# One 8 MB K load per group into a buffer of three 32 KB thirds, with P·V one group later, in a decode attention kernel

## The chip, the core and the metric

The kernel runs on one NeuronCore of a Trainium2 chip. Five engines execute their own instruction lists and meet at semaphores: TensorE (PE: matmuls, with PEld its weight loads), VectorE (DVE), ScalarE (ACT), GpSimd (POOL) and SyncE (SP), which here only starts transfers. Sixteen DMA engines move data between HBM and the on-chip memory SBUF (128 partitions); TensorE writes to PSUM. The metric is the device time of one execution in microseconds (us); lower is better.

## The reference

One decode step for 8 sequences (`B`), model width 576, 32 heads of 128 channels, a cache of 4096 keys and values per head, in bf16. An attention branch and an MLP branch are mixed by a gate:

```python
q = (x @ wq).reshape(B, Sq, H, Dh)                       # 576 -> 32*128, Sq = 1
scores = einsum("bhqd,bhkd->bhqk", q, k_cache) * (Dh ** -0.5)
p = softmax(scores); o = einsum("bhqk,bhkd->bhqd", p, v_cache)
a = o.reshape(B, Sq, H * Dh) @ wo                        # 4096 -> 576
b = gelu(layernorm(x) @ w1 + b1) @ w2 + b2               # 576 -> 4608 -> 576
g = sigmoid((x * gate_w).sum(-1)); out = g * a + (1 - g) * b
```

K and V are 8 x 32 x 4096 x 128 bf16 values each, 268 MB each; the weights are some 20 MB together. Every byte of them is used once.

## The kernel before

**Groups.** The 256 pairs (sequence, head) are worked in 32 groups (`NG`) of 8 heads of one sequence. In a group, partition p holds 256 consecutive keys (`NTT`) of one head: 16 partitions (`RH`) per head, and 256 keys x 128 channels x 2 bytes = 64 KB per partition, contiguous in HBM. So K of a group is 128 rows of 64 KB, 8 MB, and V the same.

**A group's work.** `scores` goes through 8 chunks of 32 keys (`CT`). `mult` (line 443) multiplies a chunk of K by the broadcast query on DVE into one of two buffers `p1`; eight matmuls with the identity (lines 454 and 179) add the products up in PSUM to 16 partial sums per key; `reduce` (line 461) adds those on DVE into `s_sb`. `softmax` takes the maximum on DVE (lines 478 to 486), the exponential on ACT (`E`, line 487), spreads it over the 8 heads into `P` (line 490), and sums it (lines 493 and 494). On PE, `total` (line 511) adds the sums over partitions, and `pv` (line 504, 64 matmuls) multiplies `P` by V. `evict` (line 516) copies the result by ACT, `gather` (line 522) folds it on PE, `norm` (lines 527 and 528) divides on DVE, and `put` (line 436) stores it for the output projection.

**Buffers.** `KB` is two buffers of 32 KB per partition, one for each half of a group's keys; `VB` holds one group's V (64 KB); `RB` (41,472 bytes) holds wq, then w2, then wo. w1 lies in `VB` until V of group 0 comes.

**Order.** Each engine's list is in the order in which the Python code appends to it (`op`; `aside` puts an instruction on the engine's second semaphore). All large loads are started by SP, in its order, and run on one DMA queue: wq, w1, both K halves of group 0, w2 (after the q projection, `p_Q`), V of group 0 (after the up projection has read w1, `p_up`). Then, in each group n, `load_k` of the two halves of group n+1, each waiting until the last `mult` on its half of group n (`k_done`), and `load_v` of group n+1, which waits until `pv` of group n is done (`v_done`). wo is loaded in group 0, after the down projection. Within group n the order on PE is `scores`, `total`, `pv`, `gather`, all of group n; `norm` of group n runs on DVE inside `scores` of group n+1. The up projection (line 542, 216 matmuls) runs on PE ahead of group 0; `act_h` (ACT and POOL, lines 549 to 557) makes `hT_sb` of it; the down projection (line 566, 144 matmuls) runs between the chunks of group 0. `Stream.emit_loop` writes groups 1 to 29 of PE and DVE as loops of one group each.

**The end.** V of the last group comes in eight parts, one of 128 keys in `KB[0]` and seven small ones in `VB`, and P·V follows them part by part; then the last quarter of the output projection (`a_proj`, line 566), the mix (line 691) and four small stores.

Of the kernel before, what the change touches and what calls it, by code (L numbers as in the profile page):

```python
# [12 lines left out]
B = 8  # L13
D = 576
# [126 lines left out]
def bass_gated_mix__mha_block_cached__mixer_channel_mlp__decode_kernel(  # L141
# [46 lines left out]
    wq_sb = view(RB, 0, [128, 4, SK])  # L188
    wq_t = view(RB, 4 * SK, [128, SK // 2])
    w1_sb = view(VB, 0, [128, 4, F])  # L190
    w1_t = view(VB, 4 * F, [128, F // 2])
    w2_sb = view(RB, 0, [128, NJ, D])
    wo_sb = view(RB, 0, [128, H, D])
# [63 lines left out]
    sK = [nc.alloc_semaphore(f"sK{i}") for i in range(2)]  # L257
    sV = nc.alloc_semaphore("sV")
    nK, nV = [0, 0], [0]
# [16 lines left out]
    def halves(w):  # L276
# [5 lines left out]
    ld_w1 = [load("sync", w1_sb, B_w1[0:512, :].rearrange("(p kt) f -> p kt f", kt=4), "ld_w1a"),  # L282
             load("sync", w1_t, halves(B_w1), "ld_w1b")]
# [9 lines left out]
    def load_k(u):  # L293
        n, s = divmod(u, NKH)
        nK[s] += 1
        src = kv_src(A_k_cache, n)[:, s * NTK:(s + 1) * NTK, :]
        k_land[u] = op("sync", lambda e: e.dma_start(KB[s][:, :, :], src), [k_done.get(u - NKH)], dma=(sK[s], 16 * nK[s]))

    def load_v(n):
        nV[0] += 1  # L300
        src = kv_src(A_v_cache, n)
        t = op("sync", lambda e: e.dma_start(VB[:, :, :], src), [v_done.get(n - 1) if n else st["p_up"]], dma=(sV, 16 * nV[0]))  # L302
        v_land[n] = [(t, VB, 0, 0, NTT)]
# [8 lines left out]
    V_LAST = (32, 32, 16, 16, 16, 8, 8)  # L312
    T_TURN = NTK + 64

    load_k(0)
    load_k(1)
# [13 lines left out]
    def blank(ps):  # L330
# [4 lines left out]
    c_selO = op("vector", lambda e: e.tensor_reduce(  # L335
        out=selO[:].rearrange("p t h -> p h t"),
        in_=bass.AP(tensor=ident, offset=0, ap=[[pstride(ident), 128], [TQ, HB], [1, TQ], [32, 4]]),
        axis=AX.X, op=ALU.add), [c_id])
# [38 lines left out]
    def untransposed(dst, col, waits):  # L377
# [9 lines left out]
    v_omg = op("vector", lambda e: e.tensor_scalar(out=stat[:, OMG_COL:OMG_COL + 1], in0=stat[:, G_COL:G_COL + 1],  # L387
                                                   scalar1=-1.0, scalar2=1.0, op0=ALU.mult, op1=ALU.add), [a_g])
    for i in range(4):
        a_g4 = aside("scalar", lambda e, i=i: e.activation(out=g4[32 * i:32 * i + B, :], in_=stat[:, G_COL:G_COL + 2],  # L390
                                                        func=ACT.Copy), [v_omg, c_g4])
# [6 lines left out]
    for half in range(2):  # L398
        for h in range(4):
            for kt in range(NKT):  # L400
                o = tr_ps[half][32 * h:32 * h + B, :]
                at = (kt * SK + half * (SK // 2) if kt < NKF else NKF * SK) + h * DH
                r = bass.AP(tensor=RB, offset=at, ap=[[pstride(RB), 128], [4 * DH, 4], [1, DH]])
# [8 lines left out]
    last = NG - 1  # L412
    AP = 30
    LOOP = {"tensor": 1, "vector": 1}
# [24 lines left out]
    def mult(n, c):  # L439
        u, par = n * NKH + c // NCK, c % 2  # L440
        t0 = (c % NCK) * CT
        qb = bass.AP(tensor=q_n, offset=0, ap=[[pstride(q_n), 128], [0, CT], [1, DH]])
        v_mult[n, c] = op("vector", lambda e: e.tensor_tensor(  # L443
            out=p1[:, par, :, :], in0=KB[u % NKH][:, t0:t0 + CT, :], in1=qb, op=ALU.mult),
            [k_land[u], a_q[n], p_sum.get((n, c - 2) if c >= 2 else (n - 1, c + NC - 2))]
            + ([v_yT, p_yT, p_Q] if n == 0 and c < 2 else []))
        if c % NCK == NCK - 1:
            k_done[u] = v_mult[n, c]
        for i in range(NCH):
            r = bass.AP(tensor=p1, offset=p1[:, par, 0, i * CH:i * CH + 1].offset,  # L450
                        ap=[[pstride(p1), 128], [DH, CT], [1, CH]])
            w = [v_mult[n, c], v_red.get((n, c - 2) if c >= 2 else (n - 1, c + NC - 2)), *a_Q] if i == 0 else ()
            if i == 0:
                fn = lambda e, r=r: e.matmul(tr_ps[par][:, :], lhsT=ident[:, :], rhs=r, start=True, stop=False)  # L454
            else:
                fn = lambda e, r=r, i=i: held(e, tr_ps[par][:, :], ident[:, :], r, i == NCH - 1)
            p_sum[n, c] = op("tensor", fn, w)

    def reduce(n, c):
        par = c % 2  # L460
        v_red[n, c] = op("vector", lambda e: e.tensor_reduce(  # L461
            out=s_sb[:, c * CT:(c + 1) * CT], in_=tr_ps[par][:, :].rearrange("p (t c) -> p t c", c=CH),
            axis=AX.X, op=ALU.add), [p_sum[n, c], a_exp.get(n - 1)])
# [71 lines left out]
    def up_proj(j0, j1):  # L535
        for jt in range(j0, j1):
            for kt in range(NKF + 2):
# [3 lines left out]
                w = bass.AP(tensor=VB, offset=at, ap=[[pstride(VB), 128], [NJ, n]])  # L541
                st["p_up"] = aside("tensor", lambda e, w=w, o=o, kt=kt: e.matmul(  # L542
# [3 lines left out]
    def act_h():  # L546
        hb, t2 = (up[:, i, :] for i in range(2))
        b1b = bass.AP(tensor=b1_sb, offset=0, ap=[[pstride(b1_sb), 128], [1, NJ], [0, B]])
        t = aside("scalar", lambda e: e.activation(out=hb, in_=up_ps[:, 0:NJ * B], func=ACT.Copy), [st["p_up"]])
# [6 lines left out]
        t = aside("scalar", lambda e: e.activation(out=t2, in_=t2, func=ACT.Sigmoid, scale=gelu_c), [t])  # L556
# [6 lines left out]
    def quarters(lhsT, w, first, stop, waits):  # L563

        for i in range(4):
            last = aside("tensor", lambda e, i=i: e.matmul(  # L566
                y_ps[32 * i:32 * i + B, 0:QN], lhsT=lhsT, rhs=w[:, i * QN:(i + 1) * QN], start=first, stop=stop),
                waits if i == 0 else ())
        return last
# [7 lines left out]
    def down_proj(j0, j1):  # L577
        for jt in range(j0, j1):
            st["p_down"] = quarters(hT_sb[:, jt, :], w2_sb[:, jt, :], jt == 0, jt == NJ - 1,
                                    [st["ld_w2"], st["v_h"], c_yps] if jt == 0 else ())  # L580

    def b_out():
        st["a_bx"] = aside("scalar", lambda e: e.activation(
            out=bmg_sb[0:QP, :], in_=y_ps[0:QP, 0:QN], func=ACT.Copy), [st["p_down"], st["v_h"]])
# [7 lines left out]
    def load_wo():  # L592
        st["ld_wo"] = load("sync", wo_sb, A_wo.rearrange("(h d) n -> d h n", d=128), "ld_wo", [st["p_down"]])
# [25 lines left out]
    done_a = [0]  # L619
    for b in range(B):  # L620
        q_of(b)
        if b == 0:
            q_group(0)
        up_proj(b * NJ // B, (b + 1) * NJ // B)
    act_h()
    load_w2()
    load_v(0)
    for n in range(NG):
        for e, l0 in LOOP.items():
            if l0 <= n <= AP:  # L630
                S.marks.setdefault(e, []).append(len(S.ops[e]))

        def between(c, n=n):
            if c == 1 and 1 <= n < last:
                norm(n - 1)
            if n == last and c == NCK:
                load_v_part(n, KB[0], 0, 0, NTK, [k_done[NKH * n]])
                t0 = NTK
                for nt in V_LAST:
                    load_v_part(n, VB, t0 - NTK, t0, t0 + nt, [p_pv[n - 1]])  # L640
                    t0 += nt
            if n == 0 and 3 <= c <= 6:
                down_proj((c - 3) * NJ // 4, (c - 2) * NJ // 4)
            if n >= AP and c % NCK == 2 and done_a[0] < NHG - 1:
                a_proj(done_a[0])
                done_a[0] += 1

        scores(n, between)
        if n < last:
            q_group(n + 1)  # L650
        softmax(n)
        if n < last:
            total(n)
        if n < last - 1:
            load_k(NKH * (n + 1))
            load_k(NKH * (n + 1) + 1)
            pv(n, (0,))
            evict(n)
            gather(n)
            if n == 0:  # L660
                b_out()
                load_wo()
            if n + 1 < last - 1:
                load_v(n + 1)
        if n == last - 2:
            load_v_part(last - 1, VB, 0, 0, NTK, [v_done[n]])
        if n == last - 1:
            load_k(NKH * last)
            load_k(NKH * last + 1)
            load_v_part(n, VB, NTK, NTK, NTT, [v_done[n - 1]])  # L670
            pv(n, (0,))
# [3 lines left out]
    pv(last - 1, (1,))  # L675
    evict(last - 1)
    gather(last - 1)
    norm(last - 1)
# [7 lines left out]
    pv_turned(last, range(4, 1 + len(V_LAST)))  # L686
    norm_turned(last)
    while done_a[0] < NHG:
        a_proj(done_a[0])
        done_a[0] += 1  # L690
# [48 lines left out]
```

## Time and profile before

| | us |
|---|---|
| median of 3 runs | 1302.52 (1301.04 to 1302.96) |
| the profiled execution: its time | 1302.29 |
| its span, first to last instruction | 1299.1 |
| DVE busy | 849.8 (65%) |
| PE busy | 813.6 (63%) |
| ACT busy | 68.7 (5%) |
| moved | 557.14 MB, mean 429 GB/s |

The time is 3.2 us above the span, so a change of the span is read as a change of the time. The profile gives for each engine its busy time, for each DMA queue the packets, bytes and the time that its packets took as a share of sixteen engines' span, and for each group of instructions (line, engine, operation, tile) the busy time, the mean of one and what ended the idle time before it. A row of the timeline has its start in us from the span's start, its length, the engine, the line, what is written and read, a count, and in brackets the engine's idle time before it and what ended that.

### The profile page before, as it was taken

To read this page: it belongs to the slowest core of one execution; us is meant where nothing else is said; L and a number is where in the kernel's file an instruction comes from. 1 tells how busy PE (TensorE), PEld (TensorE's weight loads), DVE (VectorE), ACT (ScalarE), POOL (GpSimd) and SP (SyncE) were. 2 spreads that over 40 slices of the span, in tenths; PEclk is the share of its full clock that TensorE was granted. 3 is DMA by queue.
4 is the path that set the end of the run, shared out by engine and by line. 5 is a ranking of instruction groups with operands and counts; after the bars stand their busy time and mean duration, and the time that the engine had idled before them with its cause. 6 is when DMAs were issued, how large, how long until landed. Compare 5 with 4: busy or idle time off the path is not lost.

```text
span 1299.1 us, 10783 instructions
## 1 busy us (share of the span) xinstructions
PE 813.6 (63%) x5020; PEld 166.9 (13%) x3228; DVE 849.8 (65%) x1073; ACT 68.7 (5%) x158; POOL 6.1 (0%) x19
## 2 busy tenths in 40 slices
PE   3963666566666565756665765665665566666667
PEld 2410111100111110111110111110011110011112
DVE  1455666677666668666668666668766667766685
ACT  3100000000000000000000000000000000000000
POOL 0100000000000000000000000000000000000000
PEclk8678877888877898888889888889878888978888
DMA  9999999999999999999999999999999999999997
GB/s 405 434 418 422 447 426 438 418 435 435 438 438 428 425 435 434 442 428 430 430 433 433 438 430 440 421 434 429 440 438 426 435 424 435 436 434 438 419 434 335
DMA packets 20124, 557.14 MB, mean 429 GB/s; under 512 B 2048, under 2 KB 6160, under 8 KB 7056
## 3 DMA queue, kind: packets, MB, share of 16 engines
q1 hardware_dynamic: 19840, 556.94, 99.7%
q8 instruction: 8, 0.13, 0.0%
q10 hardware_dynamic: 272, 0.04, 0.0%
q14 instruction: 4, 0.03, 0.0%
HBM read 556.96 MB, written 0.01 MB: 429 GB/s over the span
## 4 chain that ended last, share of the span: by engine, by line
DMA 67%; DVE 18%; PE 11%; issue 3%; SPq 0%; DVEq 0%; ACT 0%
DMA KB<-in_A_k_cache_dram 63%; DVE p L443 15%; PE psb L179 7%; DVE s_sb L461 2%; DMA VB<-in_B_w_dram 2%; DMA VB<-in_A_v_cache_dram 2%; PE psb L542 2%; PE psb L454 1%; DVEq L134 0%; SPq L262 0%; PE psb L504 0%; PE psb L421 0%; SPq L302 0%; DVE P L490 0%; PE psb L566 0%
## 5 line engine op out<-in xcount | busy, mean ns | idle before, releaser
L443 DVE TENSOR_TENSOR p<-KB,q_n 128x4096 bf16<-128x4096 bf16 x256 | 581.9, 2283 | 310.5 <-DMA KB<-in_A_k_cache_dram 301.5
L179 PE MATMUL psb<-p,ident 128*128 128x512 bf16 x1792 | 483.9, 415 | 0.0
L454 PE MATMUL psb<-p,ident 128*128 128x512 bf16 x256 | 110.7, 433 | 270.8 <-DVE p L443 270.7
L461 DVE TENSOR_REDUCE s_sb<-psb 128x32 f32<-128x512 f32 x256 | 175.2, 684 | 92.7 <-PE psb L179 92.7
L504 PE MATMUL psb<-VB,P 128*32 128x512 bf16 x1984 | 177.0, 535 | 12.0 <-DMA VB<-in_A_v_cache_dram 12.0
L454 PEld LDWEIGHTS psb<-p,ident 128*128 128x128 bf16 x256 | 26.1, 102 | 723.8 <-DVE p L443 633.4
L511 PE MATMUL psb<-rs,ones 128*128 128x8 f32 x64 | 18.9, 368 | 155.3 <-DVE rs L494 155.3
L504 PEld LDWEIGHTS psb<-VB,P 128*32 128x32 bf16 x1984 | 64.5, 129 | 110.9 <-issue 94.7
L490 DVE TENSOR_SCALAR P<-E,own 128x256 bf16<-128x256 bf16 x248 | 51.9, 284 | 17.9 <-ACT E L487 17.9
L522 PE MATMUL psb<-selO,O_sb 128*128 128x8 f32 x256 | 33.9, 259 | 22.8 <-ACT O_sb L516 22.8
L511 PEld LDWEIGHTS psb<-rs,ones 128*128 128x128 f32 x64 | 15.9, 308 | 212.0 <-DVE rs L494 211.3
L431 ACT ACTIVATE q_n<-q_bc 128x128 bf16<-128x128 bf16 x32 | 9.9, 309 | 551.1 <-DVE p L443 551.1
L522 PEld LDWEIGHTS psb<-selO,O_sb 128*128 128x128 f32 x256 | 31.0, 191 | 38.2 <-ACT O_sb L516 38.2
L516 ACT ACTIVATE O_sb<-psb 128x512 f32<-128x512 f32 x32 | 19.1, 596 | 275.6 <-PE psb L504 275.6
L487 ACT ACTIVATE E<-s_sb,mD 128x256 bf16<-128x256 f32 x32 | 16.2, 507 | 145.4 <-DVE mD L486 145.4
L542 PE MATMUL psb<-yT_sb,VB 128*128 128x8 bf16 (+1 forms) x216 | 20.1, 230 | 6.0 <-issue 6.0
L542 PEld LDWEIGHTS psb<-yT_sb,VB 128*128 128x128 bf16 (+1 forms) x216 | 18.4, 166 | 10.4 <-issue 9.3
L436 ACT ACTIVATE OT_sb<-O_n 128x8 bf16<-128x8 bf16 x31 | 7.4, 237 | 212.0 <-DVE O_n L528 212.0
L478 DVE TENSOR_REDUCE mA<-s_sb 128x1 f32<-128x256 f32 x32 | 13.4, 420 | 1.1
L493 DVE TENSOR_REDUCE es<-E 128x1 f32<-128x256 bf16 x32 | 13.2, 411 | 0.0
L494 DVE TENSOR_SCALAR rs<-own,es 128x8 f32<-128x8 f32 x32 | 7.4, 231 | 1.1
L373 PE MATMUL psb<-ident,p 8*128 8x8 bf16 x12 | 0.7, 168 | 11.7 <-ACT p L366 11.7
(75 smaller groups left out, 102.2 us busy)
## 6 DMA issues: line engine op xcount, KB each, us to landing
KB<-in_A_k_cache_dram SPq DMA_DIRECT2D x64, 4096.0 KB, 26.8
VB<-in_A_v_cache_dram SPq DMA_DIRECT2D x2, 4096.0 KB, 24.1
RB<-in_B_w_dram SPq DMA_DIRECT2D x1, 5184.0 KB, 40.2
VB<-in_B_w_dram SPq DMA_DIRECT2D x1, 4608.0 KB, 23.9
RB<-in_A_wo_dram SPq DMA_DIRECT2D x1, 4608.0 KB, 39.7
RB<-in_A_wq_dram SPq DMA_DIRECT2D x1, 4096.0 KB, 12.6
KB<-in_A_v_cache_dram SPq DMA_DIRECT2D x1, 4096.0 KB, 15.9
VB<-in_A_v_cache_dram SPq DMA_DIRECT2D x2, 1024.0 KB, 19.0
```

Source lines behind the costliest of these rows:

```text
L179: return e.add_instruction(mybir.InstMatmult(name=nc.get_next_instruction_name(), engine=mybir.EngineType.PE, ins=[e.lower_ap(rhs), e.lowe ...
L443: v_mult[n, c] = op("vector", lambda e: e.tensor_tensor(out=p1[:, par, :, :], in0=KB[u % NKH][:, t0:t0 + CT, :], in1=qb, op=ALU.mult), [k_ ...
L454: fn = lambda e, r=r: e.matmul(tr_ps[par][:, :], lhsT=ident[:, :], rhs=r, start=True, stop=False)
L461: v_red[n, c] = op("vector", lambda e: e.tensor_reduce(out=s_sb[:, c * CT:(c + 1) * CT], in_=tr_ps[par][:, :].rearrange("p (t c) -> p t c" ...
L478: t = op("vector", lambda e: e.tensor_reduce(out=mA[:, 0:1], in_=s_sb[:, :], axis=AX.X, op=ALU.max), [v_red[n, NC - 1], c_mA])
L487: a_exp[n] = op("scalar", lambda e: e.activation(out=E[:, :], in_=s_sb[:, :], func=ACT.Exp, bias=mD[:, 0:1], scale=1.0), [v_nm[n], v_P.get ...
L490: v_P[n] = op("vector", lambda e, h=h: e.tensor_scalar(out=(P if n < NG - 1 else P_last)[:, :, h, :], in0=E[:, :].rearrange("p (q t) -> p ...
L504: p_pv[n] = op("tensor", lambda e, o=o, tq=tq, at=at, buf=buf: e.matmul(o, lhsT=(P if n < last else P_last)[:, tq, :, :].rearrange("p h t ...
L511: p_z[n] = op("tensor", lambda e: e.matmul(oz_ps[:, HB:2 * HB], lhsT=ones[:, :], rhs=rs[:, :], start=True, stop=True), [v_rs[n], v_norm.ge ...
L516: a_ev[n] = op("scalar", lambda e: e.activation(out=O_sb[:].rearrange("p t d -> p (t d)"), in_=o_ps[n // last][:, :], func=ACT.Copy), [p_p ...
L522: p_oz[n] = op("tensor", lambda e, tt=tt: e.matmul(o, lhsT=O_sb[:, tt, :], rhs=selO[:, tt, :], start=(tt == 0 and n < last), stop=(tt == T ...
L542: st["p_up"] = aside("tensor", lambda e, w=w, o=o, kt=kt: e.matmul(o, lhsT=w, rhs=yT_sb[:, kt, :], start=(kt == 0), stop=(kt >= NKF)), [*l ...
```

## The change

- **K buffer.** `KB` and `RB` become one tensor `KR`: three thirds of 32 KB, of which the third one is the first part of the region of 41,472 bytes. K of group n is one load of 8 MB, 64 KB per partition, into two neighbouring thirds: thirds 0 and 1 for odd n and for n = 0, thirds 1 and 2 for the other even n (`k_base`). Third 1 is shared by all groups; `scores` reads the half that lies there first (`k_order`), and `load_k(n + 1)` waits for the last `mult` on it. Group 0 is still loaded in two halves.
- **V and P one group later.** In group n PE runs `scores(n)`, then `total`, `pv` and `gather` of group n-1; `load_v(n)` waits for `pv(n - 1)`. DVE runs `softmax(n)`, then `norm(n - 1)`; on ACT `evict(n - 1)` stands ahead of the exponential of group n.
- **The head.** SP starts wq, the two K halves of group 0, then w1. wq lies in `VB`, w1 in the region behind thirds 0 and 1, w2 in `VB` behind the first 88 tokens. V of group 0 comes in two loads: the first 88 tokens after `p_Q`, the other 168 after the down projection. The up projection, `act_h` and the down projection follow `scores(0)` on PE, in one piece each.
- **The end.** wo is loaded after the last `mult` of group 30 into the region where w1 was; the first three quarters of `a_proj` run after `scores(31)`. V of group 31 comes in the same eight parts, but into thirds 0 and 1, after the last `mult` of group 31.
- **Loops.** PE's loop covers groups 1 to 30, DVE's loop the same in turns of two groups.

```diff
-    KB = [sb(f"KB{i}", [128, NTK, DH], BF16) for i in range(NKH)]
+    THIRD = NTK * DH
+    RB0 = 2 * THIRD
+    KR = sb("KR", [128, RB0 + 9 * F // 2], BF16)
     VB = sb("VB", [128, NTT, DH], BF16)
-    RB = sb("RB", [128, 9 * F // 2], BF16)
...
+    V_AHEAD = 88
+    w2_sb = view(VB, V_AHEAD * DH, [128, NJ, D])
+    wo_sb = view(KR, RB0, [128, H, D])
+    VL = view(KR, 0, [128, NTT, DH])
...
+    def k_base(n):
+        return THIRD if n % 2 == 0 and n > 0 else 0
+    def k_order(n):
+        return (n % 2, 1 - n % 2)
+    def load_k(n):
+        nK[0] += 1
+        waits = [k_done[0, 1]] if n == 1 else [k_done[n - 1, k_order(n - 1)[0]], st["p_up"]]
+        dst = view(KR, k_base(n), [128, NTT, DH])
+        t = op("sync", lambda e: e.dma_start(dst, kv_src(A_k_cache, n)), waits, dma=(sK, 16 * nK[0]))
+        k_land[n, 0] = k_land[n, 1] = t
...
-    load_k(0)
-    load_k(1)
+    load_k_half(0, 0)
+    load_k_half(0, 1)
+    ld_w1 = [load("sync", w1_sb, ...
...
-    LOOP = {"tensor": 1, "vector": 1}
+    LOOP = {"tensor": 1, "vector": 2}
...
     def load_wo():
-        st["ld_wo"] = load("sync", wo_sb, A_wo.rearrange("(h d) n -> d h n", d=128), "ld_wo", [st["p_down"]])
+        st["ld_wo"] = load("sync", wo_sb, A_wo.rearrange("(h d) n -> d h n", d=128), "ld_wo", [k_done[last - 1, 1]])
...
         scores(n, between)
         if n < last:
             q_group(n + 1)
+            load_k(n + 1)
+        if n == 0:
+            load_v(0, 0, V_AHEAD, [p_Q])
+            up_proj(0, NJ)
+            softmax(0)
+            act_h()
...
+            down_proj(0, NJ)
+            b_out()
+            load_v(0, V_AHEAD, NTT, [st["p_down"]])
+            continue
+        if n == last - 1:
+            load_wo()
+        total(n - 1)
+        if n == last:
+            for hg in range(NHG - 1):
+                a_proj(hg)
+        pv(n - 1, (0,))
+        evict(n - 1)
+        gather(n - 1)
+        if n < last:
+            load_v(n)
         softmax(n)
...
+        norm(n - 1)
...
+    for nt in V_LAST:
+        load_v_part(last, VL, t0, t0, t0 + nt, [k_done[last, 0]])
```

More of the change, by code (lines that the diff above doesn't have):

```diff
@@ L255, in bass_gated_mix__mha_block_cached__mixer_channel_mlp__decode_kernel @@
     YT_COL = 64
-    sK = [nc.alloc_semaphore(f"sK{i}") for i in range(2)]
+    sK = nc.alloc_semaphore("sK")
     sV = nc.alloc_semaphore("sV")
-    nK, nV = [0, 0], [0]
+    nK, nV = [0], [0]
     def load(engine, dst, src, name, waits=()):
@@ L310, in load_v_part @@
         v_land.setdefault(n, []).append((t, buf, at - t0, t0, t1))
-    V_LAST = (32, 32, 16, 16, 16, 8, 8)
+    V_LAST = (128, 32, 32, 16, 16, 16, 8, 8)
     T_TURN = NTK + 64
-    load_k(0)
-    load_k(1)
+    last = NG - 1
+    load_k_half(0, 0)
+    load_k_half(0, 1)
+    ld_w1 = [load("sync", w1_sb, B_w1[0:512, :].rearrange("(p kt) f -> p kt f", kt=4), "ld_w1a"),
+             load("sync", w1_t, halves(B_w1), "ld_w1b")]
     def memset(engine, ap, value):
@@ L460, in reduce @@
         par = c % 2
+        at = (k_order(n)[c // NCK] * NCK + c % NCK) * CT
         v_red[n, c] = op("vector", lambda e: e.tensor_reduce(
-            out=s_sb[:, c * CT:(c + 1) * CT], in_=tr_ps[par][:, :].rearrange("p (t c) -> p t c", c=CH),
+            out=s_sb[:, at:at + CT], in_=tr_ps[par][:, :].rearrange("p (t c) -> p t c", c=CH),
             axis=AX.X, op=ALU.add), [p_sum[n, c], a_exp.get(n - 1)])
@@ L561, in load_w2, with quarters @@
         st["ld_w2"] = load("sync", w2_sb, B_w2.rearrange("(p j) n -> p j n", j=NJ), "ld_w2", [p_Q])
-    def quarters(lhsT, w, first, stop, waits):
+    def quarters(lhsT, w, first, stop, waits, end=aside):
         for i in range(4):
-            last = aside("tensor", lambda e, i=i: e.matmul(
+            last = (end if i == 3 else aside)("tensor", lambda e, i=i: e.matmul(
                 y_ps[32 * i:32 * i + B, 0:QN], lhsT=lhsT, rhs=w[:, i * QN:(i + 1) * QN], start=first, stop=stop),
@@ L616, in norm_turned @@
             [p_oz[n], v_rz[n]])
[L619 to L625, printed above, removed]
+    q_of(0)
+    q_group(0)
     load_w2()
-    load_v(0)
     for n in range(NG):
-        for e, l0 in LOOP.items():
-            if l0 <= n <= AP:
+        for e, turn in LOOP.items():
+            if n >= 1 and (n - 1) % turn == 0:
                 S.marks.setdefault(e, []).append(len(S.ops[e]))
         def between(c, n=n):
[L634 to L646, printed above, removed]
+            if n == 0 and c + 1 < B:
+                q_of(c + 1)
         scores(n, between)
@@ L650, in bass_gated_mix__mha_block_cached__mixer_channel_mlp__decode_kernel @@
             q_group(n + 1)
-        softmax(n)
[L652 to L671, printed above, removed]
+            load_k(n + 1)
[4 more added lines that the diff above has]
+            act_h()
+            c_selO = op("vector", lambda e: e.tensor_reduce(
+                out=selO[:].rearrange("p t h -> p h t"),
+                in_=bass.AP(tensor=ident, offset=0, ap=[[pstride(ident), 128], [TQ, HB], [1, TQ], [32, 4]]),
+                axis=AX.X, op=ALU.add), [c_id])
+            v_omg = op("vector", lambda e: e.tensor_scalar(out=stat[:, OMG_COL:OMG_COL + 1], in0=stat[:, G_COL:G_COL + 1],
+                                                           scalar1=-1.0, scalar2=1.0, op0=ALU.mult, op1=ALU.add), [a_g])
+            for i in range(4):
+                a_g4 = aside("scalar", lambda e, i=i: e.activation(out=g4[32 * i:32 * i + B, :], in_=stat[:, G_COL:G_COL + 2],
+                                                                func=ACT.Copy), [v_omg, c_g4])
+            down_proj(0, NJ)
[13 more added lines that the diff above has]
+            load_v(n)
+        softmax(n)
+        norm(n - 1)
         if n == last - 4:
@@ L674, in bass_gated_mix__mha_block_cached__mixer_channel_mlp__decode_kernel @@
             b_gate()
[L675 to L678, printed above, removed]
+    t0 = 0
+    for nt in V_LAST:
+        load_v_part(last, VL, t0, t0, t0 + nt, [k_done[last, 0]])
+        t0 += nt
     pv(last, (0,))
@@ L685, in bass_gated_mix__mha_block_cached__mixer_channel_mlp__decode_kernel @@
     gather(last)
-    pv_turned(last, range(4, 1 + len(V_LAST)))
+    pv_turned(last, range(4, len(V_LAST)))
     norm_turned(last)
-    while done_a[0] < NHG:
-        a_proj(done_a[0])
-        done_a[0] += 1
+    a_proj(NHG - 1)
     t = op("vector", lambda e: e.scalar_tensor_tensor(
```

66 lines of the change are left out of this document (27 added, 39 removed).

## The prediction

> **What bounds the kernel now.** I read the profile's page first for the shares and the DMA queue, then one row over 25 groups of the steady part, then the DMA rows of stretches in which only K or only V is in flight, then one group's timeline.
>
> ```profile
> span 1299.1 us, 10783 instructions
> ...
> q1 hardware_dynamic: 19840, 556.94, 99.7%
> ...
> DMA 67%; DVE 18%; PE 11%; issue 3%; SPq 0%; DVEq 0%; ACT 0%
> ...
> L443 DVE TENSOR_TENSOR p<-KB,q_n 128x4096 bf16<-128x4096 bf16 x256 | 581.9, 2283 | 310.5 <-DMA KB<-in_A_k_cache_dram 301.5
> ...
> L542 PE MATMUL psb<-yT_sb,VB 128*128 128x8 bf16 (+1 forms) x216 | 20.1, 230 | 6.0 <-issue 6.0
> ...
> KB<-in_A_k_cache_dram SPq DMA_DIRECT2D x64, 4096.0 KB, 26.8
> ...
> VB<-in_A_v_cache_dram SPq DMA_DIRECT2D x30, 31.5
> ```
>
> The load queue's packets fill 99.7% of sixteen engines' span. DVE's `mult` waits 301.5 us for K. A K half takes 26.8 us from issue to landing, and V 31.5.
>
> ```profile
> core 0: us, PE busy (x) PEld busy (x) DVE busy (x) ACT busy (x) POOL busy (x), PEclk, DMA share, GB/s
> 256.70:1226.10 969.40, 608.88 (x3450) 108.92 (x2050) 660.10 (x825) 41.27 (x100) 1.15 (x2) 0.85 1.00 433
> ```
>
> These 969.40 us are 25 groups (100 ACT instructions, four a group): 38.776 us a group, the DMA engines at a share of 1.00 and 433 GB/s. PE has 24.4 us of matmuls a group and DVE 26.4. So the transfers bound the kernel: a change of the other engines' work is worth nothing here by itself, and what counts is the time that the queue's packets take, and whether the queue ever runs dry.
>
> **The packets: the only term of the sum.** K comes in 32 KB packets (a half's row of a partition), V in 64 KB ones. 128 rows over 16 engines make 16 K and 8 V packets per engine and group. Three stretches with only K in flight, then three with only V, 15 us each:
>
> ```profile
> DMA packets 217, 6.59 MB, mean 439 GB/s; under 512 B 16, under 2 KB 16, under 8 KB 16
> ...
> q1 hardware_dynamic: 217, 6.59, 102.0%
> ```
>
> ```profile
> q1 hardware_dynamic: 218, 6.62, 102.5%
> ```
>
> ```profile
> q1 hardware_dynamic: 210, 6.36, 98.5%
> ```
>
> ```profile
> q1 hardware_dynamic: 96, 6.29, 96.9%
> ```
>
> ```profile
> q1 hardware_dynamic: 97, 6.36, 97.9%
> ```
>
> (One V row stands for two stretches that read alike.) 15 us of 16 engines are 240 us. K: 1.020, 1.025 and 0.985 of that are 727.2 us, for 217+218+210 packets less 16 tiny ones each, the completion writes: 597, so 1.2181 us each. V: 2 x 232.56 + 234.96 us for 289, 2.4224 us each. Two K packets cost 2.4362, one V packet of the same bytes 2.4224: 14 ns less. Checked against the clock: 16 x 1.2181 + 8 x 2.4224 = 38.869 us for a period of 38.776, so neighbours overlap by 0.093 us over 24 packets, 3.9 ns each. With K in 64 KB packets a group has 16 of them: 16 x (2.4224 - 0.0039) = 38.696. That is 0.080 us less per group, and 31 groups (1 to 31; group 0 stays in halves) give 2.5 us. V of group 30 becomes one load and V of group 0 two, which cancels; w1, w2, wo and the last V parts keep their rows. Shares are rounded to 0.1%, so at worst each stretch is off by 0.12 us of its 240, the K packet by 0.0006 us and the V packet by 0.0012; with the overlap fitted again to the period, the saving is 1.9 to 3.1 us. I take the middle, 2.5.
>
> The Trainium skill, in "DMA: Bandwidth & Descriptors", section "Why small descriptors are slow (HBM only)", gives a fixed overhead of about 3 cycles per packet; at the 850 MHz of its section "Where 436 GB/s comes from" that is 3.5 ns, by estimate 8 x 31 x 3.5 ns = 0.9 us in place of 2.5. The rows above show about 10 ns a packet, so I go by them.
>
> **Does the queue stay fed?** Everything else in the change is free as long as each load is issued before the one ahead of it has ended. One group of before gives the times:
>
> ```profile
> 566.93 4.49 DVE L443 TENSOR_TENSOR p<-KB,q_n 128x4096 bf16<-128x4096 bf16 x2 [8.91 <-DMA KB<-in_A_k_cache_dram]
> ...
> 573.50 2.28 DVE L443 TENSOR_TENSOR p<-KB,q_n 128x4096 bf16<-128x4096 bf16 x1
> ...
> 578.61 11.53 SPq L297 DMA_DIRECT2D KB<-in_A_k_cache_dram  x2
> ...
> 587.51 2.28 DVE L443 TENSOR_TENSOR p<-KB,q_n 128x4096 bf16<-128x4096 bf16 x1
> ...
> 590.07 1.67 PE L179 MATMUL psb<-p,ident 128*128 128x512 bf16 x7
> ...
> 593.89 0.51 ACT L487 ACTIVATE E<-s_sb,mD 128x256 bf16<-128x256 f32 x1 [3.76 <-DVE mD L486]
> ...
> 596.45 0.23 DVE L494 TENSOR_SCALAR rs<-own,es 128x8 f32<-128x8 f32 x1
> ...
> 597.26 4.89 PE L504 MATMUL psb<-VB,P 128*32 128x512 bf16 x64
> ...
> 602.21 0.60 ACT L516 ACTIVATE O_sb<-psb 128x512 f32<-128x512 f32 x1 [7.81 <-PE psb L504]
> 602.86 1.06 PE L522 MATMUL psb<-selO,O_sb 128*128 128x8 f32 x8 [0.71 <-ACT O_sb L516]
> ```
>
> Count from the first `mult` of group n, when K(n) has landed. The fourth `mult` ends at 11.7 (578.61 - 566.93): SP issues K(n+1), while V(n-1), the next in the queue, lands at 19.4 (half the period). Spare: 7.7 us. PE ends the last chunk at 24.8; `total` (0.6) and `pv(n-1)` (4.9) follow at once, done by 30.3: SP issues V(n), and K(n+1) lands at 38.7. Spare: 8.4 us, and from issue to landing K should show some 27 us and V some 28. SP's list has only these two in a group, in this order, and POOL's is empty there.
>
> The moved `pv` costs DVE something: `P` has one buffer, so the spreading into it waits for `pv(n-1)`, and the exponential stands behind `evict(n-1)` on ACT: 30.3 + 0.6 + 0.5, then what takes 2.3 from the end of the exponential to that of `rs` (594.40 to 596.68), then `norm`, 0.4: DVE is free at 34.2, where it was at 29.8 (596.68). K(n+1) lands at 38.7, so the cover shrinks from 8.9 us to about 4.5, and still hides all of it. Queued behind DVE's wait is only the next `mult`; behind ACT's, the next q_n, which takes 0.3.
>
> **The head.** Loads end in this order: wq, K(0), w1, w2, K(1), V(0) part one, part two. The bytes before V(0) are those of before, in another order.
>
> ```profile
> 20.09 0.33 SPq L262 DMA_DIRECT2D RB<-in_B_w_dram  x1
> ...
> 37.81 4.49 DVE L443 TENSOR_TENSOR p<-KB,q_n 128x4096 bf16<-128x4096 bf16 x2 [25.18 <-DMA KB<-in_A_k_cache_dram]
> ...
> 50.13 0.41 ACT L549 ACTIVATE Q<-psb 128x288 f32<-128x288 f32 x1 [2.11 <-PE psb L542]
> ...
> 53.99 0.79 POOL L557 TENSOR_TENSOR hT_sb<-Q 128x288 bf16<-128x288 f32 x1 [0.55 <-ACT Q L556]
> ...
> 61.62 0.74 PE L566 MATMUL psb<-RB,hT_sb 128*8 128x144 bf16 x36
> ```
>
> K(0)'s first half landed at 37.8, behind wq (4.72 MB), w1 (5.31) and itself (4.19), which at 433 GB/s are 32.9 us; the start costs the other 4.9. After the change it follows wq: 25.5. The second half comes at 35.2, w1 at 47.5, w2 at 59.8, K(1) at 79.2, V(0)'s 88 tokens (2.88 MB) at 85.9. The last `mult` of group 0 ends at 25.5 + 22.9 = 48.4 (587.51 + 2.28 - 566.93): K(1) is issued 10 us early. The 0.6 us of `q_of` behind each chunk fit into PE's idle time, as the 0.74 of line 566 did. PE then has the whole up projection: from 50.3, with 20.1 us, to 70.4; `act_h` takes 4.7 (50.13 to 54.78): 75.1; 144 matmuls of the down projection at 0.74 per 36, to double that: 78 to 81. V(0) part two is issued then. The queue runs dry somewhat ahead of the landing at 85.9; I take 84 as an estimate. Spare: 3 to 6 us, the smallest but for DVE's. K(2) is issued at 91 to 93, with part two (5.5 MB, 12.7 us) running till 97. V(1) follows `pv(0)` at 109 to 112; K(2) ends at 117. From there it is steady.
>
> ```profile
> L487 ACT ACT_TABLE_LOAD x1 | 1.3, 1283 | 0.0
> ```
>
> The moved small work of the head (`selO` on DVE, `g4` on ACT) lies in these waits; so does one more change of ACT's table, from the exponential to the sigmoid, which falls beside POOL's operations and would put 1.3 us on the chain to part two if it didn't. DVE's loop in turns of two groups halves its jumps; DVEq has 0% of the chain above, so I give that nothing.
>
>
> **The end.** K(31) lands at 0: behind it stand wo and V(30), 13.1 MB, 30 us. The last `mult` of group 31 ends at 22.9 and frees thirds 0 and 1: 7 us spare. The eight V parts and what follows the last of them are as before:
>
> ```profile
> 1271.70 22.71 DMA VB<-in_A_v_cache_dram
> 1294.41 0.05 issue
> 1294.46 0.39 PE psb L605 x8
> ```
>
> The chain ends in the last landing before and after; `softmax(31)` ends earlier, which gains nothing.
>
> **Sum.** Span 1299.1 - 2.5 = 1296.6; time 1302.29 - 2.5 = 1299.8. The profiled execution is 0.23 below the median of the runs, so against that: 1300.0, or 0.19% less, with 0.2% (2.6 us) being about what a measurement of this kernel can tell from no change.
>
> **Rivals.** (1) The packets' extra cost is smaller than the shares say, or it is hidden by the overlap: the low end, 1.9 us, gives 1300.6, and the bound of no gain gives 1302.5. For it: the difference is 14 ns in 1.2 us. Against: all K stretches read above all V stretches per byte, and the period agrees. By the page's 3 cycles it would be 1301.6. (2) The head starves the queue: V(0) part two hangs on a chain of PE, ACT, POOL and PE behind `scores(0)`, and K(2) stands behind it on SP. It decides from the point where `p_down` comes after 84; each us past it is a us. If the chain from 50.3 (28 to 31 us) took a third longer, it would end at 87 to 91: at 91, 7 us lost, 1300.0 + 7 = 1307. For it: nothing else on PE then, so nothing hides it. Against: 20.1 us were measured under the same kind of work. (3) Steady DVE: if the moved chain takes over 38.7 instead of 34.2, every group pays: 1 us over is 30 us, 1330. For it: PE sits idle some 6 us ahead of a landing (from 32.2, after `evict` and `gather`, to 38.7) in place of 2 (from 603.92 to 605.71, which is 566.93 and a period), and its first chunks are slow after a wait: 6.57 us to the third `mult` (573.50 - 566.93), where the later five take 14.0 (587.51 - 573.50), 2.80 each. Against: were all eight chunks as slow as the first two, that would be 2.9 us more, and it needs 4.5.
>
> **Numbers.** Forecast 0.80 (own range 1298.8 to 1301.2, since the runs scatter by 1 us); rival 1 0.10; rival 2 0.07; rival 3 0.03. The forecast lies at the bound of 0.2%, so I split it 0.48 faster and 0.32 same; rival 1 is same; rivals 2 and 3 are slower. The range goes from 1298.6 to 1302.3, which takes in rival 1 and leaves out rivals 2 and 3.
>
> **What would show it.** Right: per group 38.70 us; K in 64 KB packets at 2.42 us; the load queue near 99.7% of the span; DVE's wait for K about 4.5 us a group; the last landing 2.5 us earlier. Wrong: a slice near 80 to 100 us with less than full DMA (rival 2), DVE without idle time before the first `mult` (rival 3), or a period still at 38.78 (rival 1).

## The result, and the profile after

The changed kernel takes 1298.62 us (median of 13 runs, 1298.54 to 1298.89); the kernel before took 1301.12 us in the same comparison (13 runs, 1300.67 to 1302.96). The medians lie 2.50 us (0.19%) apart; the ratio taken over all runs is 0.9979, with a 95% interval of 0.9971 to 0.9988. The prediction said 2.5 us less, but 1300.0 us, and it gave the chance of a change too small to be told 0.42.

The page of the changed kernel, the lines that answer to those of before (`mult` is now line 453, the up projection line 554), and two lines of its list of transfers:

```profile
span 1296.6 us, 10702 instructions
...
q1 hardware_dynamic: 15376, 556.93, 99.6%
...
DMA 68%; DVE 18%; PE 9%; issue 3%; SPq 0%; DVEq 0%
...
L453 DVE TENSOR_TENSOR p<-KR,q_n 128x4096 bf16<-128x4096 bf16 x256 | 582.0, 2284 | 229.3 <-DMA KR<-in_A_k_cache_dram 229.3
...
L554 PE MATMUL psb<-yT_sb,KR 128*128 128x8 bf16 (+1 forms) x216 | 19.6, 229 | 0.0
```

```profile
KR<-in_A_k_cache_dram SPq DMA_DIRECT2D x31, 27.0
VB<-in_A_v_cache_dram SPq DMA_DIRECT2D x30, 29.4
```

The queue has 4464 packets fewer (31 groups, 16 engines, and on each 8 data packets and one completion write) and still fills 99.6% of the span. K takes 27.0 us from issue to landing and V 29.4, where the prediction's times gave 27 and 28: both are still issued well ahead of their turn. The span is 2.5 us shorter than the 1299.1 of the kernel before.

SP's timeline of the changed kernel, its K and V issues in the head and two K issues 28 groups apart:

```profile
47.03 0.33 SPq L308 DMA_DIRECT2D KR<-in_A_k_cache_dram  x1
47.40 30.70 SPq L319 DMA_DIRECT2D VB<-in_A_v_cache_dram  x2
90.96 0.33 SPq L308 DMA_DIRECT2D KR<-in_A_k_cache_dram  x1
107.82 0.33 SPq L319 DMA_DIRECT2D VB<-in_A_v_cache_dram  x1
129.76 0.33 SPq L308 DMA_DIRECT2D KR<-in_A_k_cache_dram  x1
...
1213.43 0.33 SPq L308 DMA_DIRECT2D KR<-in_A_k_cache_dram  x1
```

(1213.43 - 129.76) / 28 is 38.70 us a group, as predicted, against 38.78 before. The row of 47.40 is two V issues, the second one from 77.77 to 78.10.

The chain of the changed kernel at its end:

```profile
1266.95 25.03 DMA KR<-in_A_v_cache_dram
1291.98 0.05 issue
1292.03 0.39 PE psb L619 x8
```

The last landing ends at 1291.98, where it ended at 1294.41: 2.43 us earlier, and the rest of the end, 4.6 us, is as long as it was (4.7).

### The profile page after: what moved, and what is told of

It reads as the page before. It is cut to its first block, busy times and chain, and to the rows that moved or that the text cites. A ratio compares the mean times of both kernels' runs of the same rounds, so it can differ in the third digit from the quotient of the medians.

```text
span 1296.6 us, 10702 instructions
## 1 busy us (share of the span) xinstructions
PE 742.4 (57%) x5020; PEld 151.7 (12%) x3228; DVE 849.6 (66%) x1073; ACT 68.0 (5%) x160; POOL 6.2 (0%) x19
## 3 DMA queue, kind: packets, MB, share of 16 engines
q1 hardware_dynamic: 15376, 556.93, 99.6%
## 4 chain that ended last, share of the span: by engine, by line
DMA 68%; DVE 18%; PE 9%; issue 3%; SPq 0%; DVEq 0%
DMA KR<-in_A_k_cache_dram 66%; DVE p L453 16%; PE psb L179 8%; DVE s_sb L472 2%; DMA KR<-in_A_v_cache_dram 2%; PE psb L464 2%; SPq L267 0%; DVEq L134 0%; PE psb L578 0%; PE psb L619 0%; DVE out_sb L697 0%; DVE OT_sb L628 0%
## 5 line engine op out<-in xcount | busy, mean ns | idle before, releaser
L453 DVE TENSOR_TENSOR p<-KR,q_n 128x4096 bf16<-128x4096 bf16 x256 | 582.0, 2284 | 229.3 <-DMA KR<-in_A_k_cache_dram 229.3
L515 PE MATMUL psb<-VB,P 128*32 128x512 bf16 x1984 | 114.4, 384 | 5.2 <-DMA VB<-in_A_v_cache_dram 5.2
L515 PEld LDWEIGHTS psb<-VB,P 128*32 128x32 bf16 x1984 | 50.6, 97 | 54.5 <-DMA VB<-in_A_v_cache_dram 5.3
L554 PE MATMUL psb<-yT_sb,KR 128*128 128x8 bf16 (+1 forms) x216 | 19.6, 229 | 0.0
L554 PEld LDWEIGHTS psb<-yT_sb,KR 128*128 128x128 bf16 (+1 forms) x216 | 18.4, 165 | 2.7 <-issue 1.4
L522 PEld LDWEIGHTS psb<-rs,ones 128*128 128x128 f32 x64 | 12.3, 194 | 46.0 <-issue 45.2
L522 PE MATMUL psb<-rs,ones 128*128 128x8 f32 x64 | 9.4, 219 | 0.0
```

The lines of the kernel that those rows point to most:

```text
L453: v_mult[n, c] = op("vector", lambda e: e.tensor_tensor(out=p1[:, par, :, :], in0=k, in1=qb, op=ALU.mult), [k_land[n, s], a_q[n], p_sum.ge ...
L515: p_pv[n] = op("tensor", lambda e, o=o, tq=tq, at=at, buf=buf: e.matmul(o, lhsT=(P if n < last else P_last)[:, tq, :, :].rearrange("p h t ...
L522: p_z[n] = op("tensor", lambda e: e.matmul(oz_ps[:, HB:2 * HB], lhsT=ones[:, :], rhs=rs[:, :], start=True, stop=True), [v_rs[n], v_norm.ge ...
L554: st["p_up"] = (op if end else aside)("tensor", lambda e, w=w, o=o, kt=kt: e.matmul(o, lhsT=w, rhs=yT_sb[:, kt, :], start=(kt == 0), stop= ...
```

## The experiments

My theory: the whole gain is the smaller number of packets, each of which costs a fixed time beside its bytes; the rest of the change only moves work under the transfers. The rivals: the gain comes from the rest; or it is a cost per transfer and not per packet. Then the spare times on which "free" rests, and what a measurement can tell.

### The kernel before, timed against itself

> The kernel before, unchanged, timed against itself. It shows what a measurement can tell from no change, which the prediction took as 0.2%, and whether the profiled execution's 1302.29 us stands for the usual run. If the prediction's step holds, two sets of runs of the same kernel differ by up to 2.6 us. The rival: they differ by less than 1 us, and a change of 2.5 us stands clear of the scatter. In the 13 runs shown of it nine lie between 1300.67 and 1301.20 and four between 1302.11 and 1302.96; I expect the median at 1301.1 and the upper group in a quarter to a third of the runs, with the same span in both groups or one that is about 1.2 us longer.

1301.03 us (11 runs, 1300.37 to 1302.00) against 1300.96 (27 runs, 1300.35 to 1302.12): ratio 0.9999, interval 0.9990 to 1.0008. Its span was 1298.7 us and its time 1300.86 in the profiled execution, 2.2 us apart, where the execution that the prediction used had 3.2. The rival holds: 0.2% is twice what a comparison of this kernel can tell, and 1302.29 was one of its long runs. Of these 38 times 32 lie between 1300.35 and 1301.34 and six between 1301.67 and 1302.12: long runs are there, but fewer than I expected, and the median isn't touched by them. In five of the six the span is that of the other runs (1298.7 to 1299.0; the run of 1302.00 us has 1298.8, as has one of 1300.93), so what a long run has more lies outside the span.

### K in two transfers of 32 KB rows

```diff
-        dst = view(KR, k_base(n), [128, NTT, DH])
-        t = op("sync", lambda e: e.dma_start(dst, kv_src(A_k_cache, n)), waits, dma=(sK, 16 * nK[0]))
+        W = NTT // 2
+        for i in range(2):
+            nK[0] += 1
+            dst = view(KR, k_base(n) + i * W * DH, [128, W, DH])
+            t = op("sync", lambda e, dst=dst, i=i: e.dma_start(dst, kv_src(A_k_cache, n)[:, i * W:(i + 1) * W, :]), waits, dma=(sK, 16 * nK[0]))
```

> The changed kernel, with K of groups 1 to 31 as two transfers of 32 KB rows, issued one after the other where the one of 64 KB rows stood, with the same waits and places. Everything else of the change stays. If the gain is the packets (16 of 32 KB cost 0.080 us more per group than 8 of 64 KB, 31 groups), the time is 1298.6 + 2.5 = 1301.1 us and the period 38.78 us. If the gain came from the rest of the change (order of the head, P and V one group later, the end), it stays at 1298.6.

1301.05 us (11 runs, 1300.86 to 1301.19): the gain is gone to 0.1 us, with everything else of the change in place (ratio to the kernel before 0.9999, interval 0.9990 to 1.0008). Two K issues of its SP timeline, 28 groups apart:

```profile
130.12 0.80 SPq L310 DMA_DIRECT2D KR<-in_A_k_cache_dram  x2
...
1215.97 0.80 SPq L310 DMA_DIRECT2D KR<-in_A_k_cache_dram  x2
```

That is 38.78 us a group. So the order of the head, P and V one group later and the end are worth nothing by themselves, as far as this comparison can tell (its interval is -1.3 to 1.0 us); what they do is make room for the 64 KB rows.

### K in four transfers of 16 KB rows

The same edit with `NTT // 4` and `range(4)`.

> The same with four transfers of 16 KB rows: 32 packets per engine and group in place of 8. If a packet costs a fixed amount (the predicted 0.080 us over 8 packets, 10 ns each), 24 packets more are 0.24 us per group, 7.4 us in 31 groups: 1306.0 us, period 38.94. With the 3.5 ns of the Trainium skill's estimate it would be 1301.2. If the packets don't matter, 1298.6.

1306.00 us (5 runs, 1305.88 to 1306.21), to 0.02 us what a fixed 10 ns per packet gave.

```profile
130.44 1.75 SPq L310 DMA_DIRECT2D KR<-in_A_k_cache_dram  x4
...
1220.46 1.75 SPq L310 DMA_DIRECT2D KR<-in_A_k_cache_dram  x4
```

(1220.46 - 130.44) / 28 is 38.93, 0.227 us more than in the changed kernel: 9.4 ns for each of 24 packets, and 7.0 of the 7.4 us in 31 groups. So the agreement to 0.02 us is in part luck. The 3.5 ns that the prediction estimated from the Trainium skill's page "DMA: Bandwidth & Descriptors", section "Why small descriptors are slow (HBM only)", would have been 1301.2: the measurement decides against it here.

### One V transfer that writes two runs of 32 KB

```diff
-    VB = sb("VB", [128, NTT, DH], BF16)
+    GAP = 64
+    VB = sb("VB", [128, NTT * DH + GAP], BF16)
...
+            half = [[pstride(VB), 128], [THIRD + GAP, 2], [1, THIRD]]
+            src = src.rearrange("p (s t) d -> p s (t d)", s=2)
+            dst = bass.AP(tensor=VB, offset=0, ap=half)
...
```

> The changed kernel, with a gap of 128 bytes in the V buffer between tokens 127 and 128, so that a V transfer of groups 1 to 30 is still one transfer with one completion, but writes two runs of 32 KB per partition. If the cost is per packet, 30 groups pay 0.080 us less the completion write: 1298.6 + 2.2 to 2.4 = 1300.8 to 1301.0 us. If it is per transfer, the time stays at 1298.6. If the gap brings no second packet, the profile shows V packets of 64 KB still.

1299.57 us (11 runs, 1299.36 to 1299.65): 0.95 us more, neither the 2.2 to 2.4 nor nothing. The second packet is there; queue line of its page:

```profile
q1 hardware_dynamic: 19360, 556.93, 99.7%
```

3984 packets more than the changed kernel: 8 per engine in each of 30 groups, and 9 per engine for one more load of group 0, whose second part falls on both sides of the gap. 0.95 us / 30 groups / 8 is 4.0 ns a packet, and that is close to the 3.5 ns estimated from the Trainium skill's page. So what a second packet costs within one transfer is less than half of what K in two transfers showed.

### The same, with the two runs read in the opposite order

```diff
...
+            src = bass.AP(tensor=full.tensor, offset=full.offset + THIRD, ap=[list(full.ap[0]), [-THIRD, 2], [1, THIRD]])
...
```

> The changed kernel with the 128-byte gap in the V buffer, as in the run with the gap alone, and the two 32 KB runs of a row read in the opposite order: tokens 128 to 255 first. The same packets and transfers. The gap alone cost 0.95 us, 4 ns for each of the 8 more packets, where K in two transfers cost 2.43 us, 10 ns a packet. If the difference is that a packet which goes on in HBM where the last one ended is cheaper, this run costs 2.2 to 2.4 us: 1300.8 to 1301.0. If the difference lies in the second transfer, it costs what the gap alone did: 1299.6.

1299.64 us (11 runs, 1299.48 to 1299.70), as the gap alone. My first guess, that a packet is cheaper when it goes on in HBM where the last one ended, falls. The starts of neighbouring packets on one engine in the five traces, between 200 and 1200 us of each, give the same picture (mean time from one packet's start to the next, us, and a 64 KB row made of them):

```
                               one packet   64 KB of them
64 KB, changed kernel            2.4183        2.4183
32 KB, V, one transfer (gap)     1.2112        2.4224
32 KB, V, the same, swapped      1.2112        2.4224
32 KB, K, two transfers          1.2135        2.4270
16 KB, K, four transfers         0.6111        2.4444
completion write                 0.0059
```

A second packet costs 4.1 ns where the transfer stays one, and 8.7 where it is a transfer of its own (8.7 each for the four of 16 KB too). A transfer's completion write takes 5.9 ns once on each engine, which per packet of a half is 0.7. Every packet in the halves is 2.3 ns longer, not only the first; whether that is because neighbouring packets there go to different partitions, I haven't tried. The gap was put into V and the second transfer into K; in the changed kernel the 64 KB packets of the two take the same, 2.4184 and 2.4185 us from start to start, but V in two transfers wasn't run.

### The up projection twice

```diff
             up_proj(0, NJ)
+            up_proj(0, NJ)
```

> The changed kernel with the up projection done twice in the head (216 matmuls more, 19.6 us by its own profile), which delays the end of the down projection and so the second part of V of group 0 by that much. It measures the spare in the head, which the prediction put at 3 to 6 us for the loads: the time grows by 19.6 less the spare, 13.6 to 16.6 us, to 1312.2 to 1315.2. By the changed kernel's profile the second part is issued at 77.77 and the first part's last packets end between 83.6 and 85.5, so the spare is 5 to 7 us and the time 1311 to 1313. If the queue had another 19.6 us in hand, nothing would change.

1313.80 us (4 runs, 1313.38 to 1314.19): 15.2 us more. With 19.6 us added, the spare in the head was 4.4 us, inside the predicted 3 to 6 (4.2 by the issue of the second part, which came 19.4 us later). Windows of its trace (busy time of each engine with counts, granted clock, DMA share, GB/s), in the stretch where the queue waits for the second part of V:

```profile
core 0: us, PE busy (x) PEld busy (x) DVE busy (x) ACT busy (x) POOL busy (x), PEclk, DMA share, GB/s
70.00:83.00 13.00, 13.00 (x147) 12.18 (x145) 3.17 (x2) 0.00 (x0) 0.00 (x0) 0.50 0.90 385
84.00:98.00 14.00, 8.29 (x192) 7.78 (x191) 0.32 (x1) 3.12 (x8) 3.35 (x5) 0.55 0.02 8
```

The DMA share falls to 0.02 for 14 us, and none of it comes back. The first of the sixteen engines runs out at 83.6 us, and the packets of the second part start from 98.2 on: 14.6 us without work. The first packet of each engine (42 KB) then takes 1.8 to 2.5 us in place of 1.59, and V of group 0 ends 14.8 to 15.2 us later than in the changed kernel (111.5 to 113.1 against 96.3 to 98.3, from the first engine to the last). So in this run the pause costs its length and a little more, near rival 2's price of a us for a us; a short pause is in the next experiment, and no other length was tried.

### V of group 0 in one transfer after the down projection

```diff
-            load_v(0, 0, V_AHEAD, [p_Q])
...
-            load_v(0, V_AHEAD, NTT, [st["p_down"]])
+            load_v(0, 0, NTT, [st["p_down"]])
```

> The changed kernel with V of group 0 in one transfer after the down projection, without the early 88 tokens. K(1)'s packets end between 76.9 and 78.75 on the sixteen engines, and the one transfer is issued at 77.8. If the early part is needed to keep the queue fed, engines stand still for 1 to 2 us and the time grows by that, to about 1300; if the engines that end last set the time, and those still have packets when the transfer starts, nothing is lost, and one packet less per row saves 0.08: 1298.5.

1300.72 us (11 runs, 1300.20 to 1301.00): 2.1 us more, so the early 88 tokens are needed. Windows of this kernel, in the columns of the last ones:

```profile
77.00:80.00 3.00, 0.49 (x20) 0.28 (x12) 0.39 (x1) 0.29 (x1) 0.00 (x0) 0.96 1.06 355
80.00:90.00 10.00, 7.72 (x23) 0.35 (x3) 8.43 (x6) 0.00 (x0) 0.00 (x0) 0.66 0.96 415
```

and of the changed kernel:

```profile
77.00:80.00 3.00, 0.72 (x25) 0.41 (x16) 0.56 (x1) 0.29 (x1) 0.00 (x0) 0.85 0.96 403
80.00:90.00 10.00, 6.87 (x24) 0.30 (x3) 8.69 (x6) 0.00 (x0) 0.00 (x0) 0.83 1.00 428
```

From 77 to 80 us it moves 355 GB/s where the changed kernel moves 403, and from 80 to 90 us 415 in place of 428. The transfer was issued at 77.54; its first packets start at 78.50, and they take 2.7 to 3.4 us where the next ones take 2.42. Both halves of the expectation were too simple: the engines that end last (78.57) lose it too, since all sixteen first packets are slow after the pause.

### More DVE work in the changed kernel

```diff
+        t = v_rs[n]
+        for _ in range(12):
+            t = op("vector", lambda e: e.tensor_reduce(out=es2[:, :], in_=E[:, :], axis=AX.X, op=ALU.add), [t])
...
```

> The changed kernel with twelve more sums over E on DVE in each group, behind rs, into a tile that nobody reads; each 0.41 to 0.45 us by the row of es, 4.9 to 5.4 us a group together. The prediction put DVE's cover at 4.5 us, which would make this 0.4 to 0.9 us too much, 12 to 27 us in 30 groups: 1311 to 1326. The changed kernel's profile shows 6.08 us idle ahead of a group, and by that nothing is lost: 1298.6.

1301.28 us (10 runs, 1300.27 to 1302.00): 2.7 us more, neither nothing nor 12 to 27. The groups lose nothing that counts; K issues 28 groups apart, and the sums in the chain of the last group (first and last of twelve):

```profile
131.58 0.33 SPq L309 DMA_DIRECT2D KR<-in_A_k_cache_dram  x1
...
1215.81 0.33 SPq L309 DMA_DIRECT2D KR<-in_A_k_cache_dram  x1
```

```profile
1283.74 0.43 DVE es L511
...
1288.74 0.42 DVE es L511
```

(1215.81 - 131.58) / 28 is 38.72, so twelve sums, 5.4 us a group, are covered (0.02 us a group at most, 0.6 in all). The rest is at the end. The profiled execution is the longest of the ten (1302.00 us). On its chain stand the landing of V of group 30, 2.0 us later than in the changed kernel (1273.73 against 1271.73, the last completion write), for which see the last section, and behind it the twelve sums of group 31, ahead of the last `total`. Four of the ten runs lie between 1300.27 and 1300.53 and the others between 1301.19 and 1302.00; whether the later landing is what parts them isn't shown.

> The changed kernel with eighteen such sums per group, 7.4 to 8.1 us. This is over the 6.08 us idle ahead of a group by 1.3 to 2.0 us, and with 30 groups the time should be 1338 to 1359 us. If DVE's wait is slack that other waits share, it grows by less.

With `range(18)`: 1356.38 us (4 runs, 1355.17 to 1356.62), 57.8 us more, 1.93 a group over 30 groups. Two K issues 27 groups apart:

```profile
134.40 0.33 SPq L309 DMA_DIRECT2D KR<-in_A_k_cache_dram  x1
...
1233.02 0.33 SPq L309 DMA_DIRECT2D KR<-in_A_k_cache_dram  x1
```

That is 40.69 us a group, 1.99 more than 38.70. Eighteen sums are 8.1 us, so the cover lies between 6.1 and 6.2.

### The same eighteen sums in the kernel before

> The kernel before, with the same eighteen sums per group behind rs as in the run that added them to the changed kernel. There they were 1.93 us more a group than DVE's idle time of 6.08, 57.8 us in all. Here DVE was idle 8.91 us ahead of a group, and eighteen sums are 8.0 to 8.1 us by that run: if the cover has really shrunk by the move of P and V, nothing is lost in the groups, and the time stays within 3 us of 1301.0 (the sums of the last group lie on the path of its end). If the two kernels have the same cover, it grows by some 60 us here too.

1316.13 us (4 runs, 1315.72 to 1316.98): 15.1 us more, 3 had been allowed. But the groups are free, and the loss is all at the end. K issues 27 groups apart (the later one from the wait at group 30):

```profile
153.21 11.53 SPq L298 DMA_DIRECT2D KB<-in_A_k_cache_dram  x2
...
1200.55 11.52 SPq L298 DMA_DIRECT2D KB<-in_A_k_cache_dram  x2
```

(1200.55 - 153.21) / 27 is 38.79, the period of before. In the end the sums of the last two groups, 8.1 us each, stand on the chain. So the cover did shrink: what is free in a group of the kernel before costs 1.9 to 2.0 us in a group of the changed one.

## Why the prediction was right and wrong

**Right: the sum.** 31 groups at 0.080 us were predicted. The measured fall is 2.50 us; taking the 32 KB rows back returns 2.43 us; the period went from 38.78 to 38.70 as worked out, the span of the two profiled executions from 1299.1 to 1296.6. That the spans agree to the digit is luck: over the 27 later runs of the kernel before the median of the spans is 1298.8, and over the 13 of the changed kernel 1296.7, 2.1 us less; the worst rounding of the prediction, 1.9 to 3.1, holds both. That the edit with the most lines, the head and the move of P and V, is worth nothing by itself is shown, to about 1 us, by the run with K in two transfers.

**Wrong: the base, and the bound.** Two steps failed. The step from the span to the time, "time 1302.29 - 2.5 = 1299.8" and "against that: 1300.0", put the change on a profiled execution of 1302.29 and on the median of three runs, 1302.52, and took over the 3.2 us by which that execution was longer than its span. That execution and two of the three runs were long ones: 27 later runs of the kernel have their median at 1300.96, the profile of the second measurement shows 2.2 us between span and time, and that of the changed kernel 2.0 (1298.59 and 1296.6). So not every difference of the time is one of the span here: the forecast of the span, 1296.6, was met, and 1300.0 was 1.4 us too high, and the own range of the likeliest case, 1298.8 to 1301.2, missed 1298.62 by 0.2; the wide range held it by 0.02. And the step that called 0.2% about what a measurement can tell was twice too wide: the kernel against itself reads 0.9990 to 1.0008. The predicted 2.5 us was clear of no change by that measure, and 0.42 for a change too small to tell was too much for a sum whose worst rounding gave 1.9 to 3.1. The three runs themselves, 1.9 us apart, gave no better bound; the error was to centre the absolute time on them. What makes a run long, outside the span, stays open.

**The packet, 14 ns and 3.9 ns of overlap: right in sum, wrong in kind.** The prediction ascribed the difference, 10 ns a packet after the overlap, to a packet's own cost. Somewhat less than half of it is that (4.1 ns); the rest appears only when the row is split over two transfers (8.7 ns, and 0.7 for the completion write). For this change both parts fall away together, and the windows that the prediction read held both: so the sum came out, though its reason was right only in part. The 3.5 ns estimated from the Trainium skill's 3 cycles agree with the first part (4.1 ns) and not with the second.

**The queue stays fed: right, with each issue up to 1.4 us earlier than predicted.** K(1) was predicted to be issued at 48.4 and was at 47.0; the second part of V(0) at 78 to 81, and was at 77.8; K(2) at 91 to 93, and was at 91.0; V(1) at 109 to 112, and was at 107.8. The spare of the head was 4.2 to 4.4 us against 3 to 6.

**DVE's cover: mis-sized on the safe side.** Predicted 4.5 us; by the rows of 25 groups 6.4 on average (160.2 us in all), 6.1 in the group below, and by the eighteen sums 6.1 to 6.2. The term that was off is `pv` at 4.9 us. A group of the changed kernel:

```profile
567.32 1.67 PE L179 MATMUL psb<-p,ident 128*128 128x512 bf16 x7
568.83 0.28 PE L522 MATMUL psb<-rs,ones 128*128 128x8 f32 x2
...
569.04 3.64 PE L515 MATMUL psb<-VB,P 128*32 128x512 bf16 x64
...
572.73 0.60 ACT L527 ACTIVATE O_sb<-psb 128x512 f32<-128x512 f32 x1 [5.35 <-PE psb L515]
573.22 0.50 ACT L498 ACTIVATE E<-s_sb,mD 128x256 bf16<-128x256 f32 x1
573.85 1.66 DVE L501 TENSOR_SCALAR P<-E,own 128x256 bf16<-128x256 bf16 x8 [2.74 <-ACT E L498]
...
582.49 4.49 DVE L453 TENSOR_TENSOR p<-KR,q_n 128x4096 bf16<-128x4096 bf16 x2 [6.08 <-DMA KR<-in_A_k_cache_dram]
```

`pv` now follows `scores` without a pause and takes 3.64 us, at a granted clock of 1.00 over these 3.64 us; before, it came after a wait for the softmax and took 4.89, at 0.73 on average (by its trace the clock was 0.5 from 596.4 to 599.8). `total` went from 0.59 to 0.28. The order is as predicted: DVE waits 2.74 us for the exponential, which stands behind `evict` on ACT, and is idle 6.08 ahead of K.

**The rivals.** Rival 1's cheaper packet is out: the shares were right to 0.1 us. Rivals 2 and 3 didn't happen, and their prices were right in kind: in the run with the up projection twice a us past the spare cost about a us, and in the one with eighteen sums the time grew by some 30 times what a group had over its cover.

## What to carry to other kernels

Here one DMA queue is full for 99% of the span, and with the bytes fixed, what counted was the number of packets, the transfers into which a row is split, and whether the queue ever pauses; a long edit was worth 9 to 10 ns for each packet that it took away, on each engine, and no more, and the sum could be had from two kinds of window in the trace. Work that is moved under the transfers isn't free for ever: here it took DVE's cover from 8.9 to 6.1 us a group, and the 2.0 us put on top of that cost 2.0 in every group. Put a predicted difference on the kernel's usual time, not on the few runs at hand: look at what lies between span and time in each of them, and ask first what the measurement can tell.

## What the runs showed of the hardware that I had not expected

**A queue that pauses pays more than the pause.** In the run with V of group 0 in one transfer, the sixteen first packets after the pause took 2.7 to 3.4 us in place of 2.42, and started 0.96 us after the issue. After the long pause in the run with the up projection twice it was 0.99 us, and 1.8 to 2.5 us in place of 1.59 for 42 KB. The first 32 KB packets of the changed kernel's start (wq) are alike: 1.6 to 2.1 us, where later ones take 1.21. In the run with V in one transfer 2.1 us went, though the issue came only 0.6 us after the first engine had run out (77.54 against 76.93): that engine stood for 1.6 us, and its first packet was slow besides.

**The slowest engine keeps its lag.** The completion writes of one transfer show when each of the sixteen engines is done with it. From first to last, in us, for transfers that end at the times given:

```
                         23 us   59 us   79 us   98 us   157 us   1201 us
changed kernel            0.42    1.63    1.86    1.94     1.94     1.88
with twelve sums more             1.83    3.21    3.21     4.20     4.29 (1254 us)
```

A lag, once there, stays in these two, where every engine has the same bytes to move and the queue doesn't pause; the last landing waits for the slowest. In the changed kernel with eighteen sums, where the queue pauses in every group, it falls from 3.2 us at 138 us to 0.8 at 237. In the changed kernel instruction packets of 16 KB, 1.06 to 1.11 us each on one engine, ran at 42.6, 62.7 and 77.1 us, while the lag grew. In the kernel with twelve sums more there were three of 8 KB in addition, at 63.6, 69.5 and 155.2 us, and its lag grew by 1.4 and 1.0 near those times; its last landing was 2.0 us later than the changed kernel's (1293.48 against 1291.52). That the instruction packets make the lag is argued from these times only; no run here takes them away, and the three took 0.32 to 0.38 us each, less than the lag grew by, so their own length doesn't account for it.
